# Gates as sums of three one-pass products, and attention run ahead of the FFN as a pipeline across chunks

## The chip, the cores and the metric

The kernel runs on one core of a Trainium2 chip. The metric is the device time of one execution in microseconds (us), less is better. Names: PE is TensorE's matmuls, PEld its weight loads, DVE is VectorE, ACT is ScalarE, POOL is GpSimd, SP is SyncE; "SPq" or "ACTq" in a profile line is that engine's queue of transfers. A record is one instruction in the trace; the granted clock is the share of TensorE's full clock that it was given.

## The reference

```python
def _attn_ref(q, k, v, alpha):              # each (4, 8, 768, 48), fp32
    for t in range(S):
        state = alpha[:, :, t, :, None] * state + einsum('bhd,bhe->bhde', k[:, :, t], v[:, :, t])
        y[:, :, t] = einsum('bhd,bhde->bhe', q[:, :, t], state)

def _moe_ref(x, w1, w2, w3, w_out):         # x: y as (3072, 384); w1, w2 (384, 1024)
    a = x @ w1                              # w3 (1024, 1024), w_out (1024, 384)
    b = x @ w2
    h = a * b @ w3
    return h @ w_out
```

The weights arrive in 64-bit floats. The chip has no such type, so the kernel turns each into fp32 with integer and float operations ("conversion" below).

## The kernel before

The sequence of 768 is cut into chunks of 128, 24 in all for 4 batches. In a chunk, all (t, s) pairs are one masked product, and a small state T per head carries over to the next chunk. w3 is multiplied with w_out once ("fold", into `w3o`), and x, a and b are made for three chunks at a time (384 rows, a "group"). The parts that the change touches:

```python
    def to_fp32(dst, src):                       # 12 + 8 + 16 tiles
        ...
        nc.vector.tensor_scalar(top, high, 0x000FFFFF, 0x00100000, op0=ALU.bitwise_and, op1=ALU.bitwise_or)
        nc.scalar.activation(mant, top, AF.Copy, scale=2.0 ** -20)
        nc.scalar.activation(rest, low, AF.Copy, scale=2.0 ** -52)
        nc.gpsimd.tensor_add(mant, mant, rest)
        ...                                       # exponent: DVE, ACT, DVE
        nc.gpsimd.tensor_mul(dst, mant, power.bitcast(FP32))

    def advance(n):                               # the state for the next chunk
        ...
        nc.gpsimd.tensor_mul(dec, decs[(n + 1) % 3][:, 0, :], a0[:, b, c, :])
        nc.gpsimd.tensor_mul(dec, dec, decs[n % 3][:, 1, :])
        ...                                       # T = tmp * dec, also on GpSimd

    def gate(g, f):                               # 8 groups x 8 column tiles
        ...
        for p, w in ((pa, w1), (pb, w2)):
            for kk in range(KM):                  # KM = 3
                nc.tensor.matmul(p, w[:, kk, ds(f * C, C)], xT[:, kk, :], start=(kk == 0), stop=(kk == KM - 1))
        a = work.tile([C, TG], FP32, name="a")
        nc.scalar.copy(a, pa)
        nc.vector.tensor_mul(st["ab", g][:, f, :], a, pb)
    ...
    for n in range(N):                            # N = 24 chunks
        load(n + AHEAD)
        transposed(n)
        between(n)                                # one conversion or fold; from chunk 9 on also a gate or projection
        scores(n)
        decays(n + 1)
        between(n)
        outer(n)
        between(n)
        attend(n)
        advance(n)
        between(n)
        seam(n)
        between(n)
    while fill:
        run(fill)
```

## Time and profile before

| | before |
|---|---|
| median | 669.8 us (669.55 to 670.38, 3 runs) |
| span of the profiled run | 670.5 us |
| mean granted clock | 0.933 |
| PE busy | 585.8 us (87%), 2832 matmul records |
| DVE, ACT, POOL busy | 231, 189, 140 us |

The page's slices split the span in 40; a digit is a tenth of busy time. The share over the whole span (PE 87%) is an average of two stages, so the prediction, which shows the lines, reads each stage by itself: up to 208 us conversions pass from VectorE to GpSimd and back and nine chunks of attention are done; from 208 to 665 us TensorE is always busy.

### The profile page before, as it was taken

Reading aid. Unit: us, or ns where it says so; the run is one execution under the profiler, and the core shown is the slowest. Engines: PE = TensorE matmul, PEld = TensorE weight load, DVE = VectorE, ACT = ScalarE, POOL = GpSimd, SP = SyncE. Lnnn points to the kernel's source line nnn. Section 1 sums busy time; section 2 is a strip of 40 time slices with the busy share of each in tenths; the row PEclk is TensorE's granted clock in tenths of the full one; section 3 lists DMA queues with packets and bytes.
Section 4 is the critical chain, followed back from the end, with each engine's and each line's share of the span. In section 5 each row is a group of like instructions: output and inputs, shape, how many; then the busy total and the mean of one; then the engine's idle time right before and its main releaser. Section 6 shows DMA issues by size and latency. Waiting matters only on the chain.

```text
span 670.5 us, 7537 instructions
## 1 busy us (share of the span) xinstructions
PE 585.8 (87%) x2832; PEld 372.4 (56%) x2832; DVE 231.0 (34%) x348; ACT 188.5 (28%) x333; POOL 139.5 (21%) x188
## 2 busy tenths in 40 slices
PE   3472535498799999999999999999999999999997
PEld 2261324265576666666666666665666666665554
DVE  3159776877842330231222213303303222110110
ACT  2245545655543221222212212212212122110110
POOL 1036776666740000001100100000011000000000
PEclk9995656589899999999999999999999999999999
DMA  4766676658724211222214212131110101001000
GB/s 48 124 153 165 179 191 176 178 159 240 189 59 95 60 36 45 54 56 61 72 23 95 59 36 60 20 99 26 23 48 13 47 13 36 12 13 59 13 0 35
DMA packets 134628, 51.44 MB, mean 77 GB/s; under 512 B 116545, under 2 KB 128833, under 8 KB 134593
## 3 DMA queue, kind: packets, MB, share of 16 engines
q1 hardware_dynamic: 117952, 41.47, 26.4%
q10 hardware_dynamic: 15104, 4.79, 3.0%
q0 software_dynamic: 1536, 4.72, 1.9%
q8 instruction: 22, 0.36, 0.2%
q14 instruction: 14, 0.11, 0.1%
HBM read 41.46 MB, written 9.44 MB: 76 GB/s over the span
## 4 chain that ended last, share of the span: by engine, by line
PE 62%; issue 17%; DVE 7%; POOL 5%; DMA 4%; ACT 3%; ACTq 0%; SPq 0%; POOLq 0%; DVEq 0%
PE pg L327 28%; PE po L337 14%; PE pf L317 4%; DVE mant L121 3%; PE sc L232 3%; PE y L281 3%; POOL w L131 3%; PE tp L219 2%; PE lc L195 2%; PE y L277 2%; DMA a<-in_alpha_dram 2%; PE s L245 2%; DVE power L130 2%; DMA dec<-e 1%; DVE power L128 1%
## 5 line engine op out<-in xcount | busy, mean ns | idle before, releaser
L327 PE MATMUL pg<-xT,w 128*128 128x384 f32 x768 | 257.5, 489 | 0.0
L327 PEld LDWEIGHTS pg<-xT,w 128*128 128x128 f32 x768 | 143.2, 190 | 95.6 <-issue 1.9
L337 PE MATMUL po<-w3o,ab 128*128 128x384 f32 x384 | 127.1, 488 | 0.0
L330 DVE TENSOR_TENSOR ab<-a,pg 128x384 f32<-128x384 f32 x64 | 35.5, 554 | 249.4 <-PE pg L327 239.0
L337 PEld LDWEIGHTS po<-w3o,ab 128*128 128x128 f32 x384 | 72.2, 190 | 49.0 <-issue 0.7
L329 ACT COPY a<-pg 128x384 f32<-128x384 f32 x64 | 30.6, 477 | 146.3 <-PE pg L327 129.4
L340 POOL DMA_DIRECT2D out_dram<-o x24 | 13.4, 560 | 230.3 <-ACT o L339 230.3
L232 PE MATMUL sc<-qkT 48*128 48x128 f32 x384 | 34.4, 324 | 24.2 <-ACT qkT L221 19.3
L261 POOL TENSOR_TENSOR dec<-dec,a 128x4 f32<-128x4 f32 x20 | 5.1, 255 | 237.2 <-DMA dec<-e 206.2
L210 DVE TENSOR_TENSOR qk<-kq,e 128x384 f32<-128x384 f32 x48 | 45.2, 984 | 23.1 <-ACT e L199 23.1
L199 ACT ACTIVATE e<-lc 128x384 f32<-128x384 f32 x48 | 37.7, 885 | 48.9 <-PE lc L195 48.9
L125 POOL TENSOR_TENSOR mant<-mant,rest 128x512 f32<-128x512 f32 (+1 forms) x36 | 47.0, 1306 | 16.6 <-ACT mant L122 14.4
L232 PEld LDWEIGHTS sc<-qkT 48*128 48x128 f32 x384 | 28.7, 221 | 36.0 <-ACT qkT L221 21.4
L317 PE MATMUL pf<-wo,w3T 128*128 128x384 f32 x128 | 46.3, 517 | 0.7 <-ACT w3T L312 0.7
L235 DVE TENSOR_TENSOR ms<-sc,keep 128x512 int32<-128x512 int32 x48 | 31.1, 685 | 42.0 <-PE sc L232 41.9
L131 POOL TENSOR_TENSOR w<-mant,power 128x512 f32<-128x512 f32 x28 | 38.4, 1374 | 24.6 <-DVE power L130 23.0
L339 ACT COPY o<-po 128x384 f32<-128x384 f32 x24 | 11.5, 478 | 113.1 <-PE po L337 113.1
L219 PE MATMUL tp<-ident,qk 128*128 128x128 f32 x192 | 31.1, 309 | 12.6 <-DVE qk L210 12.6
L121 DVE TENSOR_SCALAR mant<-raw 128x512 uint32<-128x512 uint32 (+1 forms) x36 | 33.2, 921 | 18.4 <-POOL w L131 12.9
L223 DVE COPY qkT<-tp 128x512 f32<-128x512 f32 x24 | 16.6, 690 | 65.9 <-PE tp L219 65.9
L281 PE MATMUL y<-ms,v 128*64 128x128 f32 x384 | 33.4, 300 | 6.5 <-DVE ms L235 6.5
L219 PEld LDWEIGHTS tp<-ident,qk 128*128 128x128 f32 x192 | 25.4, 159 | 21.0 <-issue 12.4
(44 smaller groups left out, 418.8 us busy)
## 6 DMA issues: line engine op xcount, KB each, us to landing
raw<-in_moe_w_dram SPq DMA_DIRECT2D x28, 512.0 KB, 4.2
ac<-in_alpha_dram SPq DMA_DIRECT2D x24, 192.0 KB, 4.2
kq<-in_k_dram SPq DMA_DIRECT2D x24, 192.0 KB, 3.4
kq<-in_q_dram SPq DMA_DIRECT2D x24, 192.0 KB, 3.8
v<-in_v_dram SPq DMA_DIRECT2D x24, 192.0 KB, 2.9
xd<-x ACTq DMA_DIRECT2D x48, 96.0 KB, 2.4
xT<-xd SPq DMA_DIRECT2D x8, 576.0 KB, 3.9
out_dram<-o POOLq DMA_DIRECT2D x24, 192.0 KB, 2.2
```

Of the source, the lines that this page charges most:

```text
L121: nc.vector.tensor_scalar(top, high, 0x000FFFFF, 0x00100000, op0=ALU.bitwise_and, op1=ALU.bitwise_or)
L125: nc.gpsimd.tensor_add(mant, mant, rest)
L131: nc.gpsimd.tensor_mul(dst, mant, power.bitcast(FP32))
L199: nc.scalar.activation(e[:, m].rearrange("p i d j -> p j i d"), lc.rearrange("p (j i d) -> p j i d", i=2, d=D), AF.Exp, scale=sign)
L210: nc.vector.tensor_mul(qks[n % 2][:, m, :, 0:D].rearrange("p (j i) d -> p j i d", i=2), kq[:, m].rearrange("p (j i) d -> p j i d", i=2), e ...
L219: nc.tensor.transpose(tp[:, j, :], qk[:, i, 2 * j:2 * j + 2, :], ident)
L232: nc.tensor.matmul(sc[i][:, j, :], qkT[r, 0, j, :], qkT[r, 1, j, :], start=True, stop=True)
L281: nc.tensor.matmul(y[ds(DP * i, DP), j, :], vc[:, 2 * j + i, :], ms[:, i, j, :], start=(not inter and j == 0), stop=(j == NP - 1), skip_gr ...
L317: nc.tensor.matmul(po, w3T[:, j, :], wo[:, j, :], start=(j == 0), stop=(j == KF - 1))
L327: nc.tensor.matmul(p, w[:, kk, ds(f * C, C)], xT[:, kk, :], start=(kk == 0), stop=(kk == KM - 1))
L330: nc.vector.tensor_mul(st["ab", g][:, f, :], a, pb)
L337: nc.tensor.matmul(po, ab[:, f, ds(c * C, C)], w3o[:, f, :], start=(f == 0), stop=(f == KF - 1))
```

## The change

Its intent: an fp32 matmul is two records in the trace of the kernel before (768 for 384 gate matmuls), four passes by the prediction's reading. Split each weight and each x into three values of the type float32r (FP32R in the code, fp32 at reduced precision: h, l, and a combination m), and put x @ w together from three products, each hoped to take one pass. Since the splits of w1 and w2 need three times the memory, the kernel is cut into phases that reuse it: all attention first, with only w1 and w2 converted beside it; then gates beside the conversion of w_out and w3 and the folds; then gates and projections. Attention is pipelined: in a turn the scores of chunk n, the transposes and outer product of n+1, the decays of n+2 and y of n. The core of the diff, cut where marked:

```diff
-    w1 = const.tile([C, KM, DF], FP32, name="w1")
-    w2 = const.tile([C, KM, DF], FP32, name="w2")
+    w12 = [const.tile([C, 3, KM, DF], FP32R, name=f"w{i + 1}") for i in range(2)]
 ...  (conversion: one ACT and one POOL operation replaced by one on DVE)
-        nc.scalar.activation(mant, top, AF.Copy, scale=2.0 ** -20)
-        nc.gpsimd.tensor_add(mant, mant, rest)
+        nc.vector.scalar_tensor_tensor(mant, top, 2.0 ** -20, rest, op0=ALU.mult, op1=ALU.add)
 ...  (gate weights: the split)
+        nc.scalar.activation(h, w, AF.Copy, scale=(1.0 - 2.0 ** -13) / P)
+        nc.vector.scalar_tensor_tensor(l, h.bitcast(FP32), -P, w, op0=ALU.mult, op1=ALU.add)
+        nc.vector.scalar_tensor_tensor(m, h.bitcast(FP32), P + 1.0, w, op0=ALU.mult, op1=ALU.subtract)
 ...  (gate: twice this)
+        for part in range(2):
+            for kk in range(KM):
+                nc.tensor.matmul(p1, w(part, kk), x(part, kk), start=(part == kk == 0),
+                                 stop=(part == 1 and kk == KM - 1))
+        nc.scalar.activation(t, p1, AF.Copy, scale=(1.0 + 1.0 / P) * scale)
+        for kk in range(KM):
+            nc.tensor.matmul(p2, w(2, kk), x(2, kk), start=(kk == 0), stop=(kk == KM - 1))
+        nc.vector.scalar_tensor_tensor(r, p2, -scale, t, op0=ALU.mult, op1=ALU.add)
 ...  (decays: through DRAM, on SyncE's queue, instead of straight from ScalarE's queue)
 ...  (attention)
+    for n in range(N):
+        load(n + AHEAD)
+        scores(n)
+        convert(1)
+        transposed(n + 1)
+        logs(n + 3)
+        advance(n)
+        outer(n + 1)
+        convert(1)
+        decays(n + 2)
+        convert(1)
+        attend(n)
+        load_ends(n + 2)
 ...  (then, with attention's memory freed)
+    while projected < N:
+        g, f = divmod(done, KF)
+        if done < NG * KF:
+            gate(g, f)
 ...
+        if folded < KF:
+            convert(5)
 ...  (folds; after the last of them, projections)
```

## The prediction

> **What bounds the kernel now.** I read the page's busy shares by slice first, then the busy time by stretch, then the groups of instructions by shape in a steady stretch, then the chain of waits. The slices of the page:
>
> ```profile
> PE   3472535498799999999999999999999999999997
> DVE  3159776877842330231222213303303222110110
> POOL 1036776666740000001100100000011000000000
> PEclk9995656589899999999999999999999999999999
> ```
>
> Each digit is a tenth of busy time in 16.8 us. Up to about slice 13 no engine is full: VectorE and GpSimd stand at 6 to 8 tenths and TensorE is slow as well as idle (granted clock 5 to 6 tenths). From slice 13 TensorE is full to the end. The stretches (us, then busy us and count of PE, weight loads, DVE, ACT, POOL, clock, DMA share, GB/s) give the size:
>
> ```profile
> 0.00:208.00 208.00, 128.37 (x746) 89.40 (x746) 135.16 (x189) 100.72 (x173) 107.81 (x112) 0.79 0.63 151
> 208.00:665.00 457.00, 456.66 (x2086) 282.88 (x2086) 95.88 (x160) 87.30 (x160) 31.10 (x75) 1.00 0.18 43
> ```
>
> So there are **two limits**. For 208 us the kernel does 9 of 24 attention chunks (the ninth copy of y, at 207.27 us, is the mark), all 36 weight conversions and nearly all folds of w3 with w_out. For 457 us TensorE alone decides, at full clock, and work there is worth its TensorE time. In the chain of waits, the first stretch is conversions handing over to each other:
>
> ```profile
> 66.21 1.34 POOL mant L125
> 67.62 1.38 POOL w L131
> 71.24 1.35 POOL w L131
> 72.62 1.49 DVE mant L121
> ```
>
> The second is matmuls. Their cost per instruction, from the groups by shape in 350 to 450 us (busy us, mean ns of one):
>
> ```profile
> L327 PE MATMUL pg<-xT,w 128*128 128x384 f32 x151 | 50.9, 489 | 0.0
> L337 PE MATMUL po<-w3o,ab 128*128 128x384 f32 x96 | 32.0, 488 | 0.0
> L281 PE MATMUL y<-ms,v 128*64 128x128 f32 x64 | 4.4, 279 | 0.0
> L277 PE MATMUL y<-qkT,T 128*128 128x128 f32 x32 | 4.2, 275 | 0.0
> L232 PE MATMUL sc<-qkT 48*128 48x128 f32 x56 | 4.1, 283 | 0.0
> L219 PE MATMUL tp<-ident,qk 128*128 128x128 f32 x24 | 3.1, 273 | 0.0
> ```
>
> The mean (489 ns) is a latency and overlaps its neighbour; busy time over count is the pace: 32.0/96 = 333 ns for 384 columns. The whole run has 768 gate records for 64 x 2 x 3 = 384 matmuls in the program, so one fp32 matmul is two records, 667 ns.
>
> **What the Trainium skill says.** "FP8 and Floating Point Precision", TensorE Precision Notes: true FP32 takes four passes, while FP32 reduced precision reads the 4-byte value and truncates it to about 22 bits. Four passes agree with the trace: 4 x 384 columns at the 2.4 GHz that "TensorE: Matmul & The Clock Gate" (first table) states are 640 ns against 667. That reduced precision takes one pass is my inference; this trace has none. The second page's Part 1 says that an idle TensorE falls to half clock; agrees, 0.54 in 50 to 100 us, and the 16 score matmuls take 2.08 us there against 1.09 us in the chain at 218 us. "SBUF — State Buffer", SBUF: two separate sides: VectorE's two-port operations and GpSimd share a port as an exclusive lock. Agrees in kind: the same tensor_scalar takes 0.42 us alone and 1.49 us beside a GpSimd multiply of 1.35 us.
>
> **The change part by part.**
>
> 1. Gates. Per gate tile 2 x 3 fp32 matmuls (12 records, 4.0 us) become 2 x 9 float32r matmuls. One pass of 384 columns is 160 ns; the trace's two-pass record has 333 - 320 = 13 ns over its columns, so I take 170 ns. The weight load must hide beneath it: the one-pass transposes run at 3.1/24 = 130 ns, and the two-pass products of 128 columns with a full stationary at the same 131 ns, so 130 ns looks like the pace of a full load. It fits. 18 x 0.170 = 3.06 us per gate, 64 gates: 196 us instead of 257.5, 61 us less. The added eviction is 2 ACT copies (0.48 us each by the present copy), 2 VectorE ops (0.55 each) and one GpSimd multiply (about 1.1): each below 3 us per gate, beside TensorE.
>
> 2. Attention (part 1) is no longer mixed with the FFN. TensorE work per chunk at full clock: lc 0.9, transposes 8 x 0.13 = 1.05, scores 16 x 0.073 = 1.16, y from scores 16 x 0.069 = 1.1, y from the state 16 half-width records, about 1.1, outer 16 x 0.042 = 0.67: 6.0 us. VectorE: qk in one contiguous op about 0.9, mask 2 x 0.69, tmp 0.35: 2.6 us. For 16 chunks three conversion steps are added, three quarters of a gate tile: a tile is 2 x 0.42 + 4 x 0.69 = 3.6 us plus about 1 us of lock, so 3.45 us per chunk, VectorE 6.05 us. ACT is 3.2 + 1.5 = 4.7 us. I take 7.5 us per chunk with conversion and 6.7 without, as TensorE's clock will not be quite full. Start-up: the same 9216 single values for a0 are still fetched, and chunk 1 needs them (present chunk 1 begins its state product at 37.6 us). I keep 37 us to there. Sum: 37 + 14 x 7.5 + 8 x 6.7 = 196 us.
>
> 3. The conversions of w_out and w3 (24 tiles) and the 8 folds move behind part 1, beside gates. The built order has 8 gates before the first fold on TensorE. Five steps per gate are 1.67 tiles of about 3.0 us (2.2 plus lock) plus 1.1 us of gate evictions: about 6 us of VectorE per gate against 3.06 of TensorE. VectorE bounds these: 8 gates, 47 us. Then 9 gates with 8 folds are TensorE's: 9 x 3.06 + 8 x 7.4 (8 transposes 1.05, 16 records 5.33, a copy between, 1) = 87 us.
>
> 4. The rest is TensorE's: 47 gates x 3.06 = 144; projections, unchanged, 384 x 0.333 = 128; last copy and store 5.
>
> Sum: 196 + 47 + 87 + 144 + 128 + 5 = **607 us**. I put 610, for hand-overs between the phases. Against 669.8 that is 9% less: the gates give 61 us, the pipelined start much, and the lost overlap (attention no longer fills TensorE's time beside the FFN; conversions again starve it for 8 gates) takes some of it back.
>
> **Rivals.**
>
> A. float32r is not one pass, or its weight load does not hide. Two passes, 18 x 0.333 = 6.0 us per gate: 47 x 2.9 + about 35 us more, near 780. A load of 200 ns: 3.6 us per gate, near 640. For it: no view shows a float32r matmul. Against it: the skill's wording, and three products would be senseless at two passes. I give the first 6%.
>
> B. Part 1 is bound by something else: SyncE now issues every transfer in order (loads, ends, decays, outputs; about 5 us of issue per chunk at the 0.4 to 0.6 us that one takes now), DMA share was 0.63 in the first 208 us, or a half clock makes TensorE's 6 us 11. At 10 us per chunk part 1 is 55 us longer: 665, no gain. Against it: no wait on a load is large now (ACT la on DMA ac, 7.7 us in all).
>
> C. Part 1 runs at 6 us per chunk at full clock and start-up is shorter because loads are earlier: 30 us less, 575.
>
> **Range and chances.** 610, with 565 to 660 from B and C, and from 10 ns either way on the 1152 matmuls (12 us). Faster by over 2% needs under 656: 0.84. Within 2%: 0.09. Slower: 0.07, nearly all of it A.
>
> **What would show it.** Gate matmuls: 1152 records, pace about 170 ns; over 200 breaks step 1. The last copy of y near 196 us with TensorE about 80% busy before it; past 225 means B. Between it and the first fold, some 47 us with VectorE above 85% busy and TensorE about half; if TensorE is full there, step 3 was too dear. After the last fold TensorE without gaps for about 272 us.

## The result, and the profile after

| | before | after |
|---|---|---|
| median of the runs together | 669.67 us | 614.6 us (611.63 to 615.78, 4 runs) |
| ratio | | 0.9171 (95%: 0.9136 to 0.9205) |
| span of the profiled run | 670.5 us | 609.9 us |
| mean granted clock | 0.933 | 0.936 |
| PE busy | 585.8 us | 528.6 us |
| DVE, ACT, POOL busy | 231, 189, 140 us | 262, 215, 138 us |

A ratio is the mean time of one kernel's fast runs over that of the other's of the same rounds, so it is not quite the ratio of the medians. Both numbers fall where the prediction put them: 610 us, and a ratio of 0.91.

The slices of the changed kernel's page (15.2 us each):

```profile
PE   5556668568898993897999999999999999999997
DVE  3655476546543899985413111412414215122120
POOL 1021220311311455542220111211212113022120
PEclk9668798579999996997999999999999999999999
```

There are three stages now. Up to slice 13 TensorE is between half and nine tenths busy; then comes a short stage with VectorE at 8 and 9 tenths and a dip of TensorE to 3; then TensorE is full to the end. The cut by stretches, with the copy of the last y at 207 us, the first fold at 241 us and the end of the last fold at 333 us as borders (columns: us, then busy us and count of PE, weight loads, DVE, ACT, POOL, clock, DMA share, GB/s):

```profile
0.00:41.00 41.00, 21.21 (x164) 15.08 (x166) 20.89 (x34) 16.79 (x31) 7.47 (x25) 0.76 0.85 146
41.00:163.00 122.00, 87.01 (x974) 68.41 (x972) 68.97 (x111) 57.44 (x112) 27.37 (x45) 0.84 0.78 165
163.00:207.00 44.00, 41.28 (x524) 32.48 (x525) 21.55 (x38) 22.21 (x45) 7.41 (x22) 1.00 0.73 153
207.00:229.00 22.00, 21.04 (x120) 20.39 (x118) 21.10 (x34) 12.54 (x26) 12.34 (x11) 1.00 0.46 136
229.00:241.00 12.00, 1.79 (x7) 1.40 (x8) 12.00 (x17) 5.20 (x10) 7.04 (x6) 0.65 0.50 154
241.00:333.00 92.00, 82.78 (x351) 61.37 (x350) 52.38 (x77) 37.86 (x69) 28.31 (x24) 0.93 0.24 77
333.00:610.00 277.00, 273.46 (x1248) 222.22 (x1246) 64.66 (x104) 63.35 (x125) 48.24 (x48) 1.00 0.07 25
```

All 24 chunks are done at 207 us, where the kernel before had done nine. Chunks 2 to 15, beside which gate weights are converted, take 122 us, 8.7 us each; the last eight take 44 us, 5.5 each. In the first of these two stretches no engine is full: PE 71%, DVE 57%.

The pace of the new gate matmuls is read from the sequence of TensorE's work, as the distance from one start to the next (start us, us, engine, line, names, count):

```profile
421.26 1.20 PE L350 MATMUL bank<-x,w 128*128 128x384 f32 x6
422.30 0.68 PE L355 MATMUL bank<-x,w 128*128 128x384 f32 x3
422.82 1.20 PE L350 MATMUL bank<-x,w 128*128 128x384 f32 x6
```

Nine records from 421.26 to 422.82: 1.56 us, 173 ns each, so 3.12 us per gate against the 4.02 us that 12 records of 335 ns took.

What TensorE waited for from 41 to 163 us (engine, line, waited for: us in total, times, longest):

```profile
PE bank L314 <- POOL T L291: 29.8, 7, 9.9
PE bank L235 <- ACT la L229: 2.6, 1, 2.6
PE bank L264 <- DVE qk L240: 2.6, 2, 2.3
```

L314 is the product of the state with q, L291 the state update on GpSimd. Of the 35 us in which TensorE is idle here (122 - 87), 29.8 are this one wait. The sequence of one of the seven, cut where marked with dots:

```profile
106.95 1.38 POOL L192 TENSOR_TENSOR mant<-mant,power 128x512 f32<-128x512 f32 x1 [13.47 <-DVE power L190]
...
111.21 0.68 DVE L190 SCALAR_TENSOR_TENSOR power<-raw,power 128x512 uint32<-128x512 uint32 x1
111.97 1.26 POOL L192 TENSOR_TENSOR mant<-mant,power 128x512 f32<-128x512 f32 x1 [3.64 <-DVE power L190]
113.19 0.20 POOL L289 TENSOR_TENSOR dec<-dec,a 128x4 f32<-128x4 f32 x1
113.47 0.20 POOL L290 TENSOR_TENSOR dec<-dec,dec 128x4 f32<-128x4 f32 x1
113.75 0.51 POOL L291 TENSOR_TENSOR T<-tmp,dec 128x192 f32<-128x192 f32 x1
...
114.31 1.97 PE L314 MATMUL bank<-qkT,T 48*64 48x128 f32 x16 [9.88 <-POOL T L291]
```

GpSimd's work stands here in one order, with two multiplies of conversions ahead of the state update (in five of the seven waits it is one). The second waits 3.6 us for VectorE to finish its part of the conversion. The state update stands behind it, and waits for no transfer itself: the fetch of its decays had been issued at 98.0 us (an earlier one, issued at 87.3 us, was there by 92.0). The bracket of the last line is TensorE's 9.88 us. GpSimd is 22% busy in this stretch: it is not short of time, its order is wrong.

### The profile page after: what moved, and what is told of

The parts are those of the page before. It is cut to its first block, busy times and chain, and to the rows that moved or that the text cites. A ratio compares the mean times of both kernels' runs of the same rounds, so it can differ in the third digit from the quotient of the medians.

```text
span 609.9 us, 8946 instructions
## 1 busy us (share of the span) xinstructions
PE 528.6 (87%) x3376; PEld 421.3 (69%) x3376; DVE 261.5 (43%) x410; ACT 215.4 (35%) x413; POOL 138.2 (23%) x179
## 4 chain that ended last, share of the span: by engine, by line
PE 61%; issue 11%; DVE 7%; DMA 6%; POOL 6%; SPq 5%; ACT 3%; POOLq 0%; ACTq 0%; DVEq 0%
PE bank L370 20%; PE bank L350 18%; PE bank L355 9%; PE bank L399 5%; DVE power L190 2%; PE bank L314 2%; PE bank L318 2%; POOL mant L192 2%; PE bank L300 2%; DVE power L186 2%; DMA ac<-in_alpha_dram 2%; PE bank L264 1%; SPq L253 1%; SPq L166 1%; DVE mant L189 1%
## 5 line engine op out<-in xcount | busy, mean ns | idle before, releaser
L357 DVE SCALAR_TENSOR_TENSOR r<-bank,t 128x384 f32<-128x384 f32 x128 | 70.1, 555 | 224.2 <-ACT t L353 188.5
L350 PE MATMUL bank<-x,w 128*128 128x384 f32 x768 | 162.9, 346 | 0.5 <-DVE r L357 0.5
L350 PEld LDWEIGHTS bank<-x,w 128*128 128x128 f32 x768 | 135.5, 188 | 8.8 <-DVE r L357 0.8
L365 POOL TENSOR_TENSOR ab<-r 128x384 f32<-128x384 f32 x64 | 67.1, 1049 | 273.2 <-DVE r L357 273.2
L370 PE MATMUL bank<-w3o,ab 128*128 128x384 f32 x384 | 127.4, 486 | 0.0
L370 PEld LDWEIGHTS bank<-w3o,ab 128*128 128x128 f32 x384 | 72.5, 190 | 45.1
L353 ACT ACTIVATE t<-bank 128x384 f32<-128x384 f32 x128 | 62.2, 489 | 97.7 <-PE bank L350 94.4
L355 PE MATMUL bank<-x,w 128*128 128x384 f32 x384 | 87.2, 334 | 0.0
L355 PEld LDWEIGHTS bank<-x,w 128*128 128x128 f32 x384 | 68.4, 188 | 0.0
L314 PE MATMUL bank<-qkT,T 48*64 48x128 f32 x320 | 27.1, 320 | 43.1 <-POOL T L291 43.0
L314 PEld LDWEIGHTS bank<-qkT,T 48*64 48x64 f32 x320 | 21.3, 159 | 54.7 <-POOL T L291 50.8
L399 PE MATMUL bank<-wo,w3T 128*128 128x384 f32 x128 | 48.1, 534 | 9.2 <-ACT w3T L395 9.2
L303 DVE TENSOR_TENSOR ms<-bank,keep 128x512 int32<-128x512 int32 x48 | 31.1, 685 | 39.9 <-PE bank L300 39.9
L186 DVE TENSOR_SCALAR power<-raw 128x512 uint32<-128x512 uint32 (+1 forms) x36 | 29.8, 829 | 7.0 <-POOL w L192 7.0
## 6 DMA issues: line engine op xcount, KB each, us to landing
ac<-in_alpha_dram SPq DMA_DIRECT2D x24, 192.0 KB
kq<-in_k_dram SPq DMA_DIRECT2D x24, 192.0 KB
kq<-in_q_dram SPq DMA_DIRECT2D x24, 192.0 KB
v<-in_v_dram SPq DMA_DIRECT2D x24, 192.0 KB
out_dram<-o SPq DMA_DIRECT2D x24, 192.0 KB
```

Of the source, the lines that this page charges most:

```text
L186: nc.vector.tensor_scalar(power, high, 20, 0x7FF, op0=ALU.logical_shift_right, op1=ALU.bitwise_and)
L303: nc.vector.tensor_tensor(ms[:, i].bitcast(I32), sc[i].bitcast(I32), keep_bc, op=ALU.bitwise_and)
L314: nc.tensor.matmul(y[ds(DP * i, DP), j, :], Ts[n % 2][r, j, :], qkT[r, 1, j, :], start=(j == 0), stop=False, skip_group_check=True)
L350: nc.tensor.matmul(p1, w(part, kk), x(part, kk), start=(part == kk == 0), stop=(part == 1 and kk == KM - 1))
L353: nc.scalar.activation(t, p1, AF.Copy, scale=(1.0 + 1.0 / P) * scale)
L355: nc.tensor.matmul(p2, w(2, kk), x(2, kk), start=(kk == 0), stop=(kk == KM - 1))
```

## The experiments

Each is the changed kernel with one edit, unless two are named. All outputs are right. In the table, the ratio is to the kernel before in the same rounds; the changed kernel's own is 0.9171.

| run | median us | ratio (95%) |
|---|---|---|
| gates in fp32 | 646.7 | 0.9632 (0.9616 to 0.9648) |
| attention not pipelined | 658.2 | 0.9808 (0.9777 to 0.984) |
| half columns (one look) | 678.6 | |
| gate multiply on DVE | 596.6 | 0.8886 (0.8852 to 0.8921) |
| the same again | 596.3 | 0.8882 (0.8864 to 0.8901) |
| decays on ACT's queue | 602.6 | 0.8989 (0.8954 to 0.9024) |
| both of these | 603.5 | 0.9006 (0.8952 to 0.906) |
| a0 early | 617.3 | 0.9203 (0.9178 to 0.9229) |
| w_out early | 630.8 | 0.9402 (0.9371 to 0.9434) |
| multiply on DVE, a0 and w_out early | 610.6 | 0.91 (0.9061 to 0.9138) |
| both, and w_out early on DVE | 601.1 | 0.8965 (0.8934 to 0.8995) |
| multiply on DVE, w_out early on DVE | 597.0 | 0.8889 (0.8854 to 0.8924) |

### The products undone

```diff
-    w12 = [const.tile([C, 3, KM, DF], FP32R, ...) ...]
+    w12 = [const.tile([C, KM, DF], FP32, ...) ...]
     # no split of weights or x; gate():
+        for p, w in ((pa, w12[0]), (pb, w12[1])):
+            for kk in range(KM):
+                nc.tensor.matmul(p, w[:, kk, ds(f * C, C)], x3[:, kk, :], ...)
+        nc.scalar.copy(a, pa)
+        nc.vector.tensor_mul(st["ab", g, f], a, pb)
```

> Undo of the products alone: the changed kernel with w1, w2 and x kept in fp32 and each gate tile made as before by 2 x 3 fp32 matmuls. Theory (the products give most of the gain): a gate goes from 3.12 us to 12 x 0.335 = 4.02 us on TensorE, 64 x 0.90 = 58 us longer; the splits of weights and x fall away, which can give back up to 10 us in the attention part: 660 to 673 us. Rival (the new structure gives most of it): 614 to 630 us.

Measured 646.7 us: between the two. The ratios differ by 0.0461, which is 31 us of 670, somewhat more than half of the 55 us that the change gains. (The run also drops the splits and moves the gate's last multiply to VectorE.) Why the products give 31 us and not 58 is in the stretches of this run:

```profile
0.00:208.00 208.00, 151.46 (x1651) 117.34 (x1652) 95.03 (x156) 88.40 (x174) 40.70 (x92) 0.84 0.77 159
208.00:332.00 124.00, 114.01 (x384) 68.42 (x384) 61.91 (x103) 46.50 (x84) 30.21 (x24) 0.97 0.30 96
332.00:645.00 313.00, 309.33 (x960) 181.91 (x958) 26.59 (x48) 34.74 (x73) 0.00 (x0) 1.00 0.06 21
```

Attention ends at 208 us and the last fold at 332 us, as with the products (207 and 333). Only after that is there a difference, 313 us against 277. Up to the last fold a faster gate makes TensorE wait instead: from the end of attention to the last fold it waits 20.4 us with the products (10.7 us for the first w3 conversion, 9.2 us for the copies of the transposed w3) and 10.0 us here.

### The pipelining undone

```diff
-        scores(n); convert(1); transposed(n + 1); logs(n + 3); advance(n); outer(n + 1)
-        convert(1); decays(n + 2); convert(1); attend(n); load_ends(n + 2)
+        transposed(n); convert(1); scores(n); logs(n + 2); decays(n + 1); load_ends(n + 1)
+        convert(1); outer(n); convert(1); attend(n); advance(n)
```

> Undo of the pipelining across chunks alone: in each turn the chunk's own transposes, scores, outer product, y and state update follow each other, and only the decays of the next chunk are made ahead, as in the kernel before; three chunks are loaded ahead instead of four. Gates, conversions and the rest stay as in the changed kernel. Theory (the pipelining hides the hand-overs between TensorE, ScalarE and VectorE of one chunk): each chunk is 3 to 4 us longer, the total about 75 us longer, 680 to 705 us, so that the change without it would be no gain. Rival (VectorE and GpSimd set the pace of these chunks anyway): under 635 us.

Measured 658.2 us, 43 us more than with it (ratios 0.9808 and 0.9171); the expectation was too high. The last y is copied at 259.3 us instead of 207.0: chunks 2 to 23 take 9.8 us each instead of 7.6. Almost none of these 52 us comes back later: the stages behind attention last 33, 92 and 277 us, with pipelining 34, 92 and 277. (The two profiled runs are 52 us apart, the medians 44.) The rival, that the pace is the converters' anyway, falls. In chunks 2 to 23 TensorE is idle for 57 us instead of 38; one of its waits is not among those of the changed kernel:

```profile
PE bank L300 <- ACT qkT L265: 18.1, 22, 3.1
```

This is the hand-over of the transposes from ScalarE to the scores. TensorE is also busy for 160 us instead of 129 with nearly the same number of matmuls (1515 and 1496 records), at a granted clock of 0.77 instead of 0.88: most of the loss is slower matmuls, not idle time. The two undos together cost 74 us, more than the 55 gained: the parts do not add up, and what the rest of the change costs was not tested by itself.

### The multiply of the gate conversions on VectorE

```diff
-        nc.gpsimd.tensor_mul(to, mant, power.bitcast(FP32))
+        (nc.vector if dst is None else nc.gpsimd).tensor_mul(to, mant, power.bitcast(FP32))
```

> The last multiply of each gate-weight conversion goes from GpSimd to VectorE, so that the state update does not stand behind it in GpSimd's queue. Theory (chunks 2 to 15 wait for the state update, which waits for conversions on GpSimd): these chunks go from 8.7 to about 7.2 us, the total falls by 15 to 25 us to 590 to 600. Rival (SyncE's queue of transfers sets the pace): the total stays within 5 us of 614. Second rival (VectorE is the bound of these chunks): it rises.

Measured 596.6 us, and 596.3 us in the repeat: 18 us less than the changed kernel, as the theory had it. Chunks 2 to 15 take 7.8 us each (7.2 expected), the last eight 5.4. The stretch of chunks 2 to 15 and what TensorE waited for in it:

```profile
41.00:149.00 108.00, 86.81 (x964) 67.22 (x964) 72.31 (x119) 57.45 (x112) 15.87 (x36) 0.89 0.87 187
```

```profile
PE bank L314 <- POOL T L291: 13.9, 6, 4.6
PE bank L264 <- DVE qk L240: 5.4, 3, 2.3
```

PE's busy time is the same (86.8 and 87.0 us); the wait for the state has gone from 29.8 to 13.9 us and the stretch from 122 to 108. VectorE got 3 us more work and was not the bound. **This version beats both kernels**, with one edit. What is left of the wait is, by the trace, the fetch of the decays (GpSimd waits for it before 12 of the updates in these chunks, for up to 15.2 us); the next run turns to that.

### The decays on ScalarE's queue

```diff
-        nc.sync.dma_start(out=ends[0:1], in_=e[0:1, 0])        # and three more of this kind
+        nc.scalar.dma_start(out=ends[0:1], in_=e[0:1, 0])
```

> The rows of decays are stored and fetched back by ScalarE's queue instead of SyncE's. Theory (GpSimd's order binds while conversions run, the fetch of the decays only in the last 8 chunks): little, 605 to 616 us. Rival (SyncE's in-order queue is the bound of the attention part): chunks 2 to 15 go to about 7 us, total 590 to 600 us.

Measured 602.6 us, 12 us less than the changed kernel, between the two expectations. It can't be put down to SyncE's queue alone: chunks 2 to 15 gained (7.9 us each), and the last eight could not show it (5.4), as TensorE waited only 2.6 us for the state there before. The built order of GpSimd's work also changed with this edit, to a more even one: of the 10 state updates in these chunks seven have one conversion directly ahead, two have two and one has none; of the changed kernel's 11 it is five, two and four. And a new wait has come, for the logarithm of alpha on ScalarE:

```profile
PE bank L235 <- ACT la L229: 24.8, 5, 9.4
PE bank L264 <- DVE qk L240: 2.2, 3, 1.0
```

That is TensorE from 40 to 151 us: the state wait is gone from the list, and TensorE waits 24.8 us for ScalarE instead. The longest of these waits (9.4 us, to 80.0 us) goes back to the same fetch: the decays take from 65.2 to 71.4 us to arrive, VectorE stands behind the state update with its part of a conversion, and on ScalarE `la` stands behind its own part of that conversion. The other four were not followed.

With both edits:

> The two edits that helped, together: the multiply of the gate conversions on VectorE and the rows of decays on ScalarE's queue. Theory (two different waits of the same state update: GpSimd's order in chunks 2 to 15, the fetch of the decays behind SyncE's other transfers): most of both gains, 614 - 18 - 11 = 585 us, at best 580. Rival (both take the same wait away, or ScalarE's queue is then the bound): 593 to 600 us.

Measured 603.5 us, so no gain over this one edit and worse than the multiply alone; it lies above the rival's range too, but the rival was nearer: the wait for `la` on ScalarE is there again, 18.9 us from 40 to 151 us.

### The first values fetched early

```diff
     load(0)
+    load_first()
     load(1)
+    load_a0()
     ...            # the calls after decays(1) and outer(0) removed
```

> The single values of alpha (the first rows of all chunks) are fetched after the loads of chunk 0 and 1 instead of after those of chunks 2 and 3. Theory (chunk 1 waits 10.6 us for the state, which waits for these values, queued on SyncE behind eight loads): 4 to 8 us less, 607 to 611 us. Rival (the loads of chunks 2 and 3, now 7 us later, take the place of the wait): within 2 us of 614.

Measured 617.3 us (ratio 0.9203 against 0.9171; the intervals overlap): no gain, as the rival said. y of chunk 1 is copied at 44.9 us instead of 40.7: the loads of chunks 2 and 3 and the rows of decays now come later, and up to there TensorE waits 12.1 us instead of 6.7 for logarithms of alpha. The state of chunk 1 still keeps it waiting, 7.9 us instead of 10.6, now behind two conversions on GpSimd (34.0 to 37.6 us).

### w_out converted early

```diff
-    wo = foldp.tile([C, KF, DM], FP32, name="wo")        # beside the first gates
+    wo = const.tile([C, KF, DM], FP32, name="wo")        # queued behind w1 and w2, in attention
```

> The eight tiles of w_out are converted in the last eight chunks of the attention part instead of beside the first gates. Theory (from 207 us on VectorE's conversions decide when the first fold can run, and TensorE waits 12 us for them): the wait goes, 12 to 20 us less, 595 to 603 us. Rival (what is taken from there is added to the attention part, whose last eight chunks wait for transfers of decays): 610 to 620 us.

Measured 630.8 us, 16 us worse, and neither theory foresaw that. The wait for the first fold is gone, but the last eight chunks take 8.4 us each instead of 5.5. GpSimd's sequence in them:

```profile
212.93 1.07 POOL L193 TENSOR_TENSOR wo<-mant,power 128x384 f32<-128x384 f32 x1 [15.15 <-DVE power L191]
216.09 0.99 POOL L193 TENSOR_TENSOR wo<-mant,power 128x384 f32<-128x384 f32 x1 [2.10 <-DVE power L191]
217.04 0.20 POOL L290 TENSOR_TENSOR dec<-dec,a 128x4 f32<-128x4 f32 x1
217.32 0.20 POOL L291 TENSOR_TENSOR dec<-dec,dec 128x4 f32<-128x4 f32 x1
```

It is the same order as before: two multiplies of a conversion ahead of the state update, now in the chunks that had been free of it. TensorE waits 17.4 us for T from 164 to 232 us, against 2.6 in the changed kernel's last eight chunks; the rest of the 23 us is slower work, 49.7 us busy at a granted clock of 0.80 instead of 41.3 at 1.00.

Three runs tried to get the gain without this loss. All three single edits together, with w_out's multiply still on GpSimd:

> The changed kernel with the multiply of the gate conversions on VectorE, w_out converted in the last chunks and the single values fetched early, together. If the three gains add: 614 - 18 - 14 - 5 = 577 us. If they take the same wait away twice: 590 us.

Measured 610.6 us, 14 us worse than the multiply alone. Then w_out's multiply on VectorE as well, with the decays on ScalarE's queue:

> The same two edits, and w_out converted in the last eight chunks with that multiply on VectorE too, so that no conversion stands in GpSimd's queue while the state is updated. Theory (the early conversion of w_out was slower only because its multiplies stood ahead of the state update on GpSimd, and the 12 us wait for the first fold is real): 8 to 15 us below the run with the two edits, about 575 us. Rival (the work itself, on VectorE, ScalarE and in transfers, lengthens the last chunks): not below that run.

Measured 601.1 us against 603.5 us without w_out early; the intervals (0.8934 to 0.8995, 0.8952 to 0.906) overlap, so this says little. Last, the same with the decays left on SyncE's queue:

> All multiplies of conversions in the attention part on VectorE, w_out converted in the last eight chunks, and the decays left on SyncE's queue. Theory (with nothing of the conversions in GpSimd's queue the last chunks lose less than the 12 us that the first fold gains): 3 to 10 us below the run with only the multiply moved, 587 to 594 us. Rival (the work lengthens the last chunks by as much): within 3 us of it.

Measured 597.0 us beside 596.3 us for the repeat of the multiply alone (0.8889 and 0.8882): equal, as the rival said. The transposes of the first fold start 9 us sooner than in the first run of the multiply alone (212.9 us against 222.2), and the last y comes 11 us later (202.7 us against 192.0). So the order on GpSimd was not all: with the conversions of w_out off it, the last eight chunks still take 7.2 us each instead of 5.4 (5.9 in the repeat's profile). The repeat's expectation:

> The same kernel as the run with the gate multiply on VectorE, repeated beside the other on one chip: again about 597 us, ratio 0.885 to 0.892.

### Half the columns per matmul

```diff
-                nc.tensor.matmul(p1, w(part, kk), x(part, kk), ...)
+                for h in range(2):                       # the same weights, 192 columns each
+                    r = ds(h * TG // 2, TG // 2)
+                    nc.tensor.matmul(p1[:, r], w(part, kk), x(part, kk)[:, r], ...)
```

> Each float32r gate matmul is made as two of 192 columns with the same weights, 2304 records. Theory (one pass of the columns over the array, with a weight load of about 130 ns hidden beneath the 173 ns): the pace falls only to the load, about 130 ns, so a gate takes 36 x 0.13 = 4.7 us and the total is about 100 us longer, 710 us. Rival (the pace is columns plus a small constant and the load is no limit): about 36 x 0.093 = 3.3 us per gate, 628 us.

Measured 678.6 us in one look of unknown state, 64 us more: between the two expectations. The sequence of TensorE's work late in this run:

```profile
421.56 1.50 PE L352 MATMUL bank<-x,w 128*128 128x192 f32 x12
422.89 0.83 PE L359 MATMUL bank<-x,w 128*128 128x192 f32 x6
423.57 1.50 PE L352 MATMUL bank<-x,w 128*128 128x192 f32 x12
```

18 records from 421.56 to 423.57 us: 112 ns each. If columns alone set the pace, 192 fewer of them would by an estimate take 80 ns (half of the 160 that the prediction worked out for 384) off the 173, to 93 ns. The pace stops at 112 instead, so something not halved binds there: the weight load, or another cost per record of that size, which this run does not tell apart. The Trainium skill's page "TensorE: Matmul & The Clock Gate", section LDWEIGHTS, puts a load at its columns over 1.2 GHz, 107 ns for 128; the measured pace agrees with that. A load in series with the columns would have let the whole 80 ns go, and only 61 went. So at 384 columns the load is hidden, with some 60 ns to spare, and the 130 ns that the prediction read from the transposes was too much for it.

## Why the prediction was right

The total was forecast at 610 us and measured at 614.6. By stages, the single terms were less good than their sum:

| stage | predicted us | measured us (profiled run) |
|---|---|---|
| attention, to the last y | 196 | 207 |
| to the first fold | 47 | 34 |
| the folds | 87 | 92 |
| the rest | 277 | 277 |
| sum | 607 | 610 |

**Step 1, the gates.** Right in mechanism and size: 170 ns predicted, 173 measured, 3.12 us per gate against 3.06. The sentence "the gates give 61 us" was too much: undoing the products costs 31 us. The sum did not contain the mistake: it prices the gates by stage, and up to the last fold the undo changed nothing (attention 208 us for 207, last fold at 332 for 333). The gain of a stage is to be read from that stage.

**Step 2, attention.** The total is 11 us off, and its terms more. The state product of chunk 1 begins at 36.8 us for 37, but the sum let chunk 2 follow at once, and y of chunk 1 is copied at 41. Chunks 2 to 15 took 8.7 us for 7.5, and the mechanism was another: the prediction had VectorE and TensorE about 80% busy there (6.05 and 6.0 us of 7.5), and they were 57% and 71%; TensorE waited for a state update that stood behind conversions in GpSimd's queue. Moving the conversion's multiply off that queue took 18 us out, which shows the cause. The prediction had counted GpSimd's time but not its order. The last eight chunks took 5.5 us for 6.7: with no conversion beside them TensorE is 94% busy at full clock, and a chunk's TensorE work, counted as 6.0 us, is 5.2 (41.3 us for eight).

**Step 3, conversions behind attention.** The prediction said that VectorE bounds eight gates to 6 us each. VectorE is indeed full (21.1 of 22 us, then 12.0 of 12) and sets the length of this stage, but not the pace of each gate: seven gates (not eight) run on TensorE at full pace in 22 us, ahead of their evictions on VectorE, which stand among the conversions. The last matmuls of the seventh gate and its last eviction:

```profile
227.83 0.69 PE L355 MATMUL bank<-x,w 128*128 128x384 f32 x3
238.83 0.54 DVE L357 SCALAR_TENSOR_TENSOR r<-bank,t 128x384 f32<-128x384 f32 x1
```

Meanwhile TensorE waits 10.7 us until the first w3 is converted. The stage took 34 us instead of 47: seven gates at 4.9 us, not eight at 6. Part of the difference is that the first conversions of w_out were done before it began (one complete by 202.1 us on VectorE). The folds took 92 us for 87.

**Step 4, the rest.** 277 us for 277, with 48 gates left instead of 47 (864 records of 18 per gate).

So +11, -13, +5 and 0 cancel: the range rested on terms that erred in both directions, and the closeness of the sum is partly luck. Of the rivals, A fell (173 ns, and the half-column run shows a load hidden). B, SyncE's order, was at most a part: the run that moved the decays gained 12 us, but in chunks in which GpSimd's order changed with it. How much of these 12 us belongs to SyncE stays open. B's own sum was off too: 22 chunks at 10 us are 61 us above the 159 of the forecast, not 55.

## What to carry to other kernels

When several stages have different limits, price an improvement only in the stage where its engine sets the pace: in the profiled runs the same products were worth nothing before the last fold and 36 us after it. An engine that is 22% busy can still be on the critical path: before moving cheap work to it, look at what stands in its queue behind work that waits for others. And after each edit look for the wait that took the place of the one removed: fetching a0 early and converting w_out early each went after a wait of about 11 us, and neither gained, as other waits came up.

## What the Trainium skill lacked or had wrong

- The pace of a float32r matmul: no page states it. "FP8 and Floating Point Precision" names the reduced precision without its passes. Measured: 173 ns per record of 128 x 384 with a full stationary, 112 ns at 192 columns; a true fp32 matmul of 384 columns is two records of 333 ns.
- "TensorE: Matmul & The Clock Gate", section LDWEIGHTS, gives a load as columns over 1.2 GHz, 107 ns for 128. The pace of 112 ns agrees, but the load's record in the profile lasts 188 ns and that page doesn't say that the record isn't the pace.
- "Perfetto Trace Analysis", section Identifying the Most-Contended Engine, advises the busy share of weight loads, beside the share of peak work, as a measure. Here it is 80% from 333 us on (222 of 277 us), where the half-column run shows the load to be hidden with about 60 ns to spare. In a run of gates alone it is 100% (from 421.26 to 433.22 us), and 100% too in the half-column run (421.56 to 427.59 us): it does not tell the two cases apart.
